# The first scan in two parts, the first rows from two queues, and POOL out of the heads and the last block

## The chip, the cores and the metric

The kernel runs on one core of one Trainium2 chip. The metric is the device time of one execution in microseconds; a comparison takes the median of several runs. Work is shared by five engines: PE (TensorE, matrix products, its weight loads shown as PEld), DVE (VectorE), ACT (ScalarE), POOL (GpSimd) and SP (SyncE, which in this kernel issues nearly all transfers). Each runs its own list of instructions in order and waits on semaphores for the others.

## The reference

Attention with a decay, and two feed-forward layers behind it:

```python
# q, k, v: (B 4, H 8, S 576, D 64); f: (B, H, S)
scores = scale * np.matmul(q, k.transpose(0, 1, 3, 2))
log_f = np.log(np.clip(f, 0.0001, 1.0))
cum = np.cumsum(log_f, axis=-1)
decay = cum[:, :, :, None] - cum[:, :, None, :]
scores = np.where(causal, -1000000000.0, scores + decay)
attn = np.exp(scores - np.max(scores, axis=-1, keepdims=True))
attn = attn / (np.sum(attn, axis=-1, keepdims=True) + 1e-09)
x = np.matmul(attn, v)                     # -> (2304 tokens, 512)
h = x @ moe_w_in                           # 512 x 2048
x = np.maximum(h, 0.0) ** 2 @ moe_w_out    # 2048 x 512
h = x @ moe2_w_in
g = np.where(h >= 1, h, np.where(h <= -1, 0.0, (h + 1) ** 2 / 4))
out = g @ moe2_w_out
```

The weights come as 64-bit floats; the kernel decodes them to 32-bit ones and splits each into a high and a low part, since its products are made of three matmuls (high by high, low by high, high by low).

## The kernel before

**Stages.** The tokens are cut into four blocks of columns. The first 256 rows of each sequence are "heads", computed in eight groups of four heads each by `attention32` (names with a q: s0q are the scores of group 0, E0q its exponentials, tr0q the transposed ones, av0q its second product). Groups 0 to 3 make the first block and run alone at the start, to about 48 us; groups 4 to 7 run between the feed-forward steps. The rest of each sequence is computed by `attention`, 32 tasks of one head each, between the feed-forward steps from 233 to 665 us. A feed-forward step is 24 matmuls of 128x512 of the first layer (L1129) or the second (L1180 to L1182). The last block of 768 tokens is computed by `last_block` with fewer products than the plain way: it makes sums of the weights and differences of the activations first. It does the first layer pair (mo=0) from 665 to 787 us and the second (mo=1) from 787 to the end. In each, eight pairs of activation chunks follow each other (names like G1_2: layer pair 1, chunk pair 2), 36 matmuls and more each.

**Start.** `setup` loads f (32 heads by 576), clips it (L535), takes the logarithm (L537) and sums it along the row with one scan (L538). The first 256 columns of all sums go to memory as `cumd` (L550). A group's tile QK holds queries and keys in 64 rows and the sums in two rows more, which the score matmul takes in with the rest. Those two rows of group 0 are copied straight from the scan's tile by `first_rows` (L554, two transfers); those of the other groups are read from `cumd` (L669). QK is cleared ahead of that (L606); K and Q of the later tasks are cleared at L564 and L565, by POOL or DVE. PE meanwhile runs 34 warm-up matmuls (L593). Behind the scores (L696) come, for each head, the row maximum and the shifted scores (L640, DVE), the exponential (L707, ACT), the sum and its reciprocal (L714, L715) and the normalising product (L730 on ACT, L731 on DVE, L732 on POOL).

**Second product of a task.** `attention` transposes its exponentials by transfers (PT), copies them to 32-bit tiles (pr) and multiplies them with V (L953): nine narrow matmuls of 320, 192 and 64 columns.

**Last block.** A pair's activations: h (L1335), ACT's two steps to r (L1354, L1356), DVE's step to G (L1359), then a split of G (gh and gl; ghl; L621, L624, L633) and subtractions of slots of G from each other (L1227, "G<-G"), and the products a, b, c (L1298 to L1300). Beside it `weight_sums` adds halves of the loaded second weights wo (wfs<-wo, twice 512 columns a pair) and makes four sums of 256 columns (sf), which are split into sum and stored. These adds go through `add`, which lets them run on DVE (L1227) or POOL (L1229):

```python
    def add(due, out, a, b, width, deps, bufs, sub=False, psum=False, slack=0.0, pool=True):
        op = ALU.subtract if sub else ALU.add
        alts = {"DVE": (dve_t(width), lambda: nc.vector.tensor_tensor(out(), a(), b(), op=op), *([] if psum else [True]))}
        if pool and not psum:
            alts["POOL"] = (pool2_t(width), lambda: nc.gpsimd.tensor_tensor(out(), a(), b(), op=op))
```

**What sets the order.** Every operation is entered with a due time, a price for each engine that may run it, what it depends on and its buffers. `Schedule.improve` simulates these lists with several weights, keeps the shortest result and fixes for every operation the engine and the place; `emit` writes the code in that order. It takes POOL's operations, and those of DVE that are marked with True, as exclusive of each other. Any changed price or due time may therefore reorder operations far away.

## Time and profile before

| | |
|---|---|
| time, three runs | 930.96, 932.15 (median), 935.03 us |
| profiled run | 933.11 us |
| its span | 931.3 us |
| mean granted clock of PE | 0.998 |
| busy in the span | PE 916.8, DVE 748.7, ACT 678.0, POOL 68.3 us |
| DMA | 247.38 MB, 266 GB/s on average |

The span reaches from the first to the last record of the profiled run; what is left to its time lies around it. A busy time is the sum of an engine's instructions. PE is the engine with next to no idle time, so a view of it is read for where it stands still; the other engines are read for what they do at those places.

### The profile page before, as it was taken

To read this page: it belongs to the slowest core of one execution; us is meant where nothing else is said; L and a number is where in the kernel's file an instruction comes from. 1 tells how busy PE (TensorE), PEld (TensorE's weight loads), DVE (VectorE), ACT (ScalarE), POOL (GpSimd) and SP (SyncE) were. 2 spreads that over 40 slices of the span, in tenths; PEclk is the share of its full clock that TensorE was granted. 3 is DMA by queue.
4 is the path that set the end of the run, shared out by engine and by line. 5 is a ranking of instruction groups with operands and counts; after the bars stand their busy time and mean duration, and the time that the engine had idled before them with its cause. 6 is when DMAs were issued, how large, how long until landed. Compare 5 with 4: busy or idle time off the path is not lost.

```text
span 931.3 us, 14313 instructions
## 1 busy us (share of the span) xinstructions
PE 916.8 (98%) x4674; PEld 799.3 (86%) x4674; DVE 748.7 (80%) x1711; ACT 678.0 (73%) x1354; POOL 68.3 (7%) x174
## 2 busy tenths in 40 slices
PE   7999999999999999999999999999999999989998
PEld 6788888877887888888888888888899999989998
DVE  8999999999858788888777778887676657788774
ACT  7998989897768777887777877886555555545553
POOL 4411001001000000000000000000000000322100
PEclk9999999999999999999999999999999999999999
DMA  7799999899898886998798888976697657756562
GB/s 216 257 356 397 347 399 332 324 359 332 295 300 249 257 273 219 320 262 236 242 295 261 279 247 236 262 218 179 205 307 266 218 219 255 253 196 225 214 226 89
DMA packets 132954, 247.38 MB, mean 266 GB/s; under 512 B 90512, under 2 KB 92720, under 8 KB 118096
## 3 DMA queue, kind: packets, MB, share of 16 engines
q1 hardware_dynamic: 132880, 246.47, 81.2%
q8 instruction: 37, 0.61, 0.3%
q14 instruction: 37, 0.30, 0.1%
HBM read 178.62 MB, written 46.84 MB: 242 GB/s over the span
## 4 chain that ended last, share of the span: by engine, by line
PE 89%; DVE 6%; ACT 2%; DMA 2%; issue 1%; SPq 0%; POOL 0%; DVEq 0%; ACTq 0%; POOLq 0%
PE h L1129 26%; PE h L1335 13%; PE acc L1180 9%; PE acc L1182 9%; PE acc L1181 9%; PE av L953 4%; PE s L847 2%; PE s L848 2%; PE b L1298 2%; PE b L1300 2%; PE b L1299 2%; PE c L1298 1%; PE c L1300 1%; PE c L1299 1%; PE a L1300 1%; PE a L1299 1%
## 5 line engine op out<-in xcount | busy, mean ns | idle before, releaser
L1129 PE MATMUL h<-x,whl 128*128 128x512 f32 x1128 | 286.1, 395 | 0.0
L1129 PEld LDWEIGHTS h<-x,whl 128*128 128x128 f32 x1128 | 208.9, 188 | 42.4 <-issue 0.5
L1180 PE MATMUL acc<-gh,whl 128*128 128x512 f32 x384 | 151.8, 395 | 0.0
L1182 PE MATMUL acc<-gl,whl 128*128 128x512 f32 x384 | 150.2, 391 | 0.0
L1181 PE MATMUL acc<-gh,whl 128*128 128x512 f32 x384 | 149.9, 390 | 0.0
L1182 PEld LDWEIGHTS acc<-gl,whl 128*128 128x128 f32 x384 | 72.1, 188 | 15.7
L1180 PEld LDWEIGHTS acc<-gh,whl 128*128 128x128 f32 x384 | 72.1, 188 | 14.6 <-issue 0.9
L881 ACT ACTIVATE E<-E,st 128x448 f32<-128x448 f32 (+2 forms) x96 | 63.5, 662 | 28.8 <-DVE st L640 22.7
L1181 PEld LDWEIGHTS acc<-gh,whl 128*128 128x128 f32 x384 | 72.2, 188 | 13.9
L633 DVE TENSOR_TENSOR gl<-g,gh 128x512 fp32r<-128x512 f32 x96 | 67.7, 706 | 15.8 <-PE acc L1182 9.9
L640 DVE CUSTOM_DVE_ANT_0 E<-s,mask 128x288 f32<-128x288 f32 (+2 forms) x128 | 59.8, 500 | 20.1 <-PE s L848 19.8
L1335 PE MATMUL h<-x_last,wi 128*128 128x384 f32 x384 | 72.7, 340 | 3.1 <-DVE G L1359 3.1
L923 DVE SCALAR_TENSOR_TENSOR PP<-E,st,PP 128x512 f16<-128x512 f32 (+2 forms) x128 | 70.0, 593 | 3.8 <-ACT PP L919 2.8
L1335 PE MATMUL h<-x,wi 128*128 128x384 f32 x384 | 72.0, 334 | 0.0
L919 ACT ACTIVATE PP<-E,st 128x512 f16<-128x512 f32 (+2 forms) x128 | 66.8, 590 | 6.9 <-DVE st L893 6.1
L1335 PEld LDWEIGHTS h<-x_last,wi 128*128 128x128 f32 x384 | 67.8, 190 | 4.3 <-DVE G L1359 4.1
L1335 PEld LDWEIGHTS h<-x,wi 128*128 128x128 f32 x384 | 67.1, 188 | 0.4
L624 DVE CAST pr<-PT 128x640 fp32r<-128x640 f16 (+2 forms) x93 | 32.0, 396 | 28.3 <-DMA PT<-PP 28.0
L1227 DVE TENSOR_TENSOR G<-G 128x384 f32<-128x384 f32 x64 | 37.7, 608 | 19.6 <-ACT G L1351 19.0
L953 PEld LDWEIGHTS av<-pr,vt 128*128 128x128 f32 x288 | 43.6, 188 | 4.1 <-ACT pr L621 1.0
L621 ACT ACTIVATE pr<-PT 128x640 fp32r<-128x640 f16 (+2 forms) x67 | 37.0, 602 | 13.4 <-DMA PT<-PP 12.3
L1156 ACT ACTIVATE r<-h,half 128x512 f32<-128x512 f32 x48 | 32.7, 681 | 18.9 <-PE h L1129 18.4
(352 smaller groups left out, 1796.7 us busy)
## 6 DMA issues: line engine op xcount, KB each, us to landing
whl<-scr SPq DMA_DIRECT2D x56, 1024.0 KB
raw<-in_w_dram SPq DMA_DIRECT2D x28, 1024.0 KB
scr<-whl SPq DMA_DIRECT2D x28, 1024.0 KB
wo<-scr SPq DMA_DIRECT2D x48, 512.0 KB
in<-in_qkv_dram SPq DMA_DIRECT2D x32, 608.0 KB
wi<-scr SPq DMA_DIRECT2D x32, 512.0 KB
whl<-scr SPq DMA_DIRECT2D x16, 512.0 KB
sum<-wfs SPq DMA_DIRECT2D x16, 512.0 KB
```

The lines of the kernel that those rows point to most:

```text
L633: alts["DVE"] = (dve_t(n), lambda: nc.vector.tensor_sub(out(), a(), b()), True)
L640: return nc.vector.tensor_tensor_reduce(out=out, in0=ps, in1=mask[:m, OFF - q0:OFF - q0 + n], scale=scale, scalar=3e38, op0=ALU.add, op1=A ...
L881: nc.scalar.activation(Ec.tile[:m, :e], Ec.tile[:m, :e], AF.Exp, scale=-1.0, bias=nmx(), accum_out=st.tile[:m, 1, ci:ci + 1])))}, [*tops, ...
L919: nc.scalar.activation(hi, x, AF.Copy, scale=r())
L923: nc.vector.scalar_tensor_tensor(lo, x, r(), hi, op0=ALU.mult, op1=ALU.subtract)
L953: nc.tensor.matmul(av.tile[:, c0:W], vt.tile[:, kc, :, :], dst()[:, i, :], start=(kc == 0 and i == 0), stop=(kc == NK - 1))
L1129: nc.tensor.matmul(ps.tile[:, :n], w.tile[:, 0, wi, kc * P:(kc + 1) * P], src.tile[:, kc, xi, :n], start=(kc == 0 and i == 0), stop=(kc == ...
L1180: nc.tensor.matmul(a.tile[:, :n], wh, gh.tile[:, :n], start=(fc == 0), stop=False)
L1181: nc.tensor.matmul(a.tile[:, :n], wl, gh.tile[:, :n], start=False, stop=False)
L1182: nc.tensor.matmul(a.tile[:, :n], wh, gl.tile[:, :n], start=False, stop=(fc == NFC - 1))
L1227: alts = {"DVE": (dve_t(width), lambda: nc.vector.tensor_tensor(out(), a(), b(), op=op), *([] if psum else [True]))}
L1335: nc.tensor.matmul(ps.tile[:, :n], W0.tile[:, j, wi, kc * P:(kc + 1) * P], src.tile[:, kc, xi, k * n:(k + 1) * n], start=(kc == 0 and i == ...
```

## The change

- Clip, logarithm and scan are each made in two parts, columns 0 to 256 and 256 to 576. The second scan starts from the last column of the first. What needs all columns (`cumhl`) hangs on the second.
- `first_rows` issues the first of group 0's two rows from SP and the second from ACT. The due time of the store to `cumd` goes from -98 to -80, behind that of the rows (-90).
- The memsets of Q and K are POOL's alone. The normalising product of the heads has no POOL any more (L732).
- `add` has no POOL any more, nor have the copies and subtractions that make x2, the input of the second layer pair in the last block (at L1405).
- The nine matmuls of a second product are sorted by width, narrow ones first but for the very first.
- The warm-up's price for the planner goes from 0.43 to 0.36 per matmul, and the planner knows a transfer by its price (a tuple), not by the engine, since ACT issues one now.

```diff
-            if e == "SP":
+            if type(cost) is tuple:
                 issue, size, hold, tail = cost
...
-            if o.eng == "SP":
+            if type(cost) is tuple:
                 end -= 0.65 + cost[0] + cost[1] + cost[3] - cost[2]
...
         sch.op(due + 90, {"POOL": (0.05, lambda: G.memset(half, 0.5))})
-        o3 = sch.op(due, {"DVE": (0.37, lambda: V_.tensor_scalar(
-            fr(), fr(), 1e-4, 1.0, op0=ALU.max, op1=ALU.min))}, [o1], [sb])
-        o4 = sch.op(due, {"ACT": (0.58, lambda: A.activation(lf(), fr(), AF.Ln))}, [o3, oh], [sb])
-        o5 = sch.op(-98.5, {"DVE": (0.67, lambda: V_.tensor_tensor_scan(
-            cum(), onesf(), lf(), 0.0, op0=ALU.mult, op1=ALU.add))}, [o4, o2], [sb])
-        sch.op(due, {"ACT": (1.4, lambda: A.activation(warm, warm, AF.Exp))}, [o4])
+        cut = [slice(0, HEAD), slice(HEAD, S)]
+        o3 = [sch.op(due, {"DVE": (0.15 + 0.1 * i, lambda c=c: V_.tensor_scalar(
+            fr()[:, c], fr()[:, c], 1e-4, 1.0, op0=ALU.max, op1=ALU.min))}, [o1], [sb]) for i, c in enumerate(cut)]
+        o4 = [sch.op(due, {"ACT": (0.32 + 0.05 * i, lambda c=c: A.activation(lf()[:, c], fr()[:, c], AF.Ln))}, [o3[i], oh], [sb])
+              for i, c in enumerate(cut)]
+        scan = lambda c, x: V_.tensor_tensor_scan(
+            cum()[:, c], onesf()[:, c], lf()[:, c], x(), op0=ALU.mult, op1=ALU.add)
+        o5 = sch.op(-98.5, {"DVE": (0.6, lambda: scan(cut[0], lambda: 0.0))}, [o4[0], o2], [sb])
+        o5b = sch.op(T_START + 14, {"DVE": (0.74, lambda: scan(cut[1], lambda: cum()[:, HEAD - 1:HEAD]))}, [o4[1], o5], [sb])
+        sch.op(due, {"ACT": (1.4, lambda: A.activation(warm, warm, AF.Exp))}, o4)
         hi = lambda: fr().bitcast(F32R)
         lo = lambda: lf().bitcast(F32R)
         o6 = sch.op(T_START + 16, {
             "ACT": (0.57, lambda: A.activation(hi(), cum(), AF.Copy)),
             "DVE": (0.37, lambda: V_.tensor_copy(hi(), cum())),
-        }, [o5], [sb], early=T_START + 12)
+        }, [o5b], [sb], early=T_START + 12)
         o7 = sch.op(T_START + 17, {"DVE": (0.67, lambda: V_.tensor_sub(lo(), cum(), fr()))}, [o6], [sb])
         o7 = [sch.op(due + 125, {"SP": (dma_t(73728), lambda i=i, b=b: nc.sync.dma_start(
             out=cumhl[:, i, :], in_=b()))}, [o], [sb], early=T_START + 12) for i, b, o in ((0, fr, o6), (1, lf, o7))]
-        o8 = sch.op(-98, {"SP": (dma_t(32768), lambda: nc.sync.dma_start(
+        o8 = sch.op(-80, {"SP": (dma_t(32768), lambda: nc.sync.dma_start(
             out=cumd, in_=cum()[:, :HEAD]))}, [o5], [sb])
 
-        def first_rows(row, out, due, deps):
-            return sch.op(due, {"SP": (dma_t(4096), lambda: nc.sync.dma_start(
+        def first_rows(row, out, due, deps, name):
+            eng = nc.sync if name == "SP" else nc.scalar
+            return sch.op(due, {name: (dma_t(4096, False), lambda: eng.dma_start(
                 out=out(), in_=cum()[row:row + QUAD, :HEAD]))}, [o5, *deps], [sb, QK[0]], early=0.0)
...
                 for r, x in ((64, 0.0), (4, -1.0 if n == "Q" else 1.0)):
-                    z = sch.op(due, {
-                        "POOL": (0.5, lambda t=t, r=r, x=x: G.memset(t[0:r, :].bitcast(F32), x)),
-                        "DVE": (0.5, lambda t=t, r=r, x=x: V_.memset(t[0:r, :].bitcast(F32), x)),
-                    }, [z])
+                    z = sch.op(due, {"POOL": (0.5, lambda t=t, r=r, x=x: G.memset(t[0:r, :].bitcast(F32), x))}, [z])
                 zs[n, i] = z
...
 
-        sch.op(-90, {"PE": (0.43 * WARM, lambda: mms(WARM))}, [id_op], [ps])
+        sch.op(-90, {"PE": (0.36 * WARM, lambda: mms(WARM))}, [id_op], [ps])
 
...
                 if i == 0:
-                    rows = [first_rows(row, lambda t=t: place(t, 0, QUAD), -90, [*cleared[0, 0], *cleared[0, 1]])
+                    rows = [first_rows(row, lambda t=t: place(t, 0, QUAD), -90, [*cleared[0, 0], *cleared[0, 1]], ("SP", "ACT")[t])
                             for t in range(2)]
...
                     "DVE": (dve2_t(e), lambda x=x, r=r: nc.vector.tensor_scalar(x(), x(), r(), None, op0=ALU.mult), True),
-                    "POOL": (pool_t(e), lambda x=x, r=r: nc.gpsimd.tensor_scalar(
-                        x(), x(), r(), 0.0, op0=ALU.mult, op1=ALU.add)),
                 }, [o_r], [Eb, st]))
...
         def mms():
-            for kc, c0, n, k, dst in moves:
-                for i in range(k):
-                    nc.tensor.matmul(
-                        av.tile[:, c0:W], vt.tile[:, kc, :, :], dst()[:, i, :],
-                        start=(kc == 0 and i == 0), stop=(kc == NK - 1))
+            parts = [(i, m) for m in moves for i in range(m[3])]
+            parts.sort(key=lambda p: (p[0] + p[1][0] > 0, p[1][2]))
+            for j, (i, (kc, c0, n, k, dst)) in enumerate(parts):
+                nc.tensor.matmul(av.tile[:, c0:W], vt.tile[:, kc, :, :], dst()[:, i, :],
+                                 start=(j == 0), stop=(j == len(parts) - 1))
 
...
 
-    def add(due, out, a, b, width, deps, bufs, sub=False, psum=False, slack=0.0, pool=True):
+    def add(due, out, a, b, width, deps, bufs, sub=False, psum=False, slack=0.0):
         op = ALU.subtract if sub else ALU.add
         alts = {"DVE": (dve_t(width), lambda: nc.vector.tensor_tensor(out(), a(), b(), op=op), *([] if psum else [True]))}
-        if pool and not psum:
-            alts["POOL"] = (pool2_t(width), lambda: nc.gpsimd.tensor_tensor(out(), a(), b(), op=op))
         return sch.op(due, alts, deps, bufs, slack)
...
                 sp1 = split(f"1_{nm}", tA + t_h + 1.5, gb, 0, [og[0, 0]], True)
-                o_t1 = add(tA + 3 * t_h + 1.5, slot(0), slot(1), slot(0), n, [og[0, 0], og[0, 1], sp1[3]], [gb], sub=True, pool=False)
-                o_t3 = add(te + 1.5, slot(1), slot(3), slot(1), n, [o_t1, og[1, 1], og[0, 1]], [gb], sub=True, pool=False)
+                o_t1 = add(tA + 3 * t_h + 1.5, slot(0), slot(1), slot(0), n, [og[0, 0], og[0, 1], sp1[3]], [gb], sub=True)
+                o_t3 = add(te + 1.5, slot(1), slot(3), slot(1), n, [o_t1, og[1, 1], og[0, 1]], [gb], sub=True)
                 sp5 = split(f"5_{nm}", te + 1.5, gb, 0, [o_t1])
-                o_t2 = add(te + 2, slot(0), slot(3), slot(0), n, [o_t1, sp5[3], og[1, 1]], [gb], sub=True, pool=False)
+                o_t2 = add(te + 2, slot(0), slot(3), slot(0), n, [o_t1, sp5[3], og[1, 1]], [gb], sub=True)
                 sp6 = split(f"6_{nm}", te + 2.5, gb, 0, [o_t2])
-                o_t4 = add(te + 3, slot(0), slot(2), slot(0), n, [o_t2, sp6[3], og[1, 0]], [gb], sub=True, pool=False)
+                o_t4 = add(te + 3, slot(0), slot(2), slot(0), n, [o_t2, sp6[3], og[1, 0]], [gb], sub=True)
                 g_op[c] = {"t4": o_t4, "t3": o_t3, "b21": og[1, 0], "b22": og[1, 1]}
...
                     o = o_r = add(due, t, ps, lambda: old.tile, n, dep, bufs, psum=True)
-                    o = sch.op(due + 0.5, copies(hi, t, n), [o], [buf, x2])
-                    x2_ops[d, k] = sch.op(due + 0.7, subs(lo, t, lambda: hi().bitcast(F32), n), [o], [buf, x2])
+                    o = sch.op(due + 0.5, copies(hi, t, n, "ACT DVE"), [o], [buf, x2])
+                    x2_ops[d, k] = sch.op(due + 0.7, subs(lo, t, lambda: hi().bitcast(F32), n, "DVE"), [o], [buf, x2])
                     return o_r
```

In the order of SP at the start (setup holds the scan's result, QK_199 is the tile of group 0, QK_237 that of group 1, raw are weights, vt values), before:

```order
L1022 DMA raw-2_228<-in_w_dram 128x512
L656 DMA QK_199<-in_qkv_dram 64x1024
L550 DMA cumd<-setup 32x256
L554 DMA QK_199<-setup 1x4x256 x2
L656 DMA QK_237<-in_qkv_dram 64x2048
L677 DMA vt0q<-in_qkv_dram 128x512
L1022 DMA raw-1_269<-in_w_dram 128x512
L669 DMA QK_237<-cumd 1x4x256 x2
L677 DMA vt1q<-in_qkv_dram 128x512
```

and after:

```order
L1022 DMA raw-2_228<-in_w_dram 128x512
L658 DMA QK_199<-in_qkv_dram 64x1024
L554 DMA cumd<-setup 32x256
L559 DMA QK_199<-setup 1x4x256
L658 DMA QK_237<-in_qkv_dram 64x2048
L679 DMA vt0q<-in_qkv_dram 128x512
L679 DMA vt1q<-in_qkv_dram 128x512
L671 DMA QK_237<-cumd 1x4x256 x2
L1022 DMA raw-1_284<-in_w_dram 128x512
```

The store to cumd stays ahead of the row; one row is left of two; raw-1 moves behind the rows of group 1.

The other row is in the order of ACT, after (before, none is there; low and wf are steps of decoding weights):

```order
L538 ACTIVATE setup<-setup 32x256
L538 ACTIVATE setup<-setup 32x320
L544 ACT_TABLE_LOAD
L544 ACTIVATE warm<-warm 128x1
L559 DMA QK_199<-setup 1x4x256
L1054 ACTIVATE low_260<-raw-2_228 128x512
```

It stands behind both logarithms, the load of the table for the exponential and its first use.

In the order of DVE at the start, from the clip to the first row maximum (L640 before, L642 after), before:

```order
L535 TENSOR_SCALAR setup<-setup 32x576
L606 MEMSET QK_199 64x2x256
L606 MEMSET QK_199 1x2x256
L538 SCALAR_TENSOR_TENSOR setup<-setup 32x576
L565 MEMSET K_0_144 64x576
L565 MEMSET K_1_145 64x576
L565 MEMSET K_0_144 4x576
L565 MEMSET K_1_145 4x576
L1065 TENSOR_SCALAR wf-2_257<-wf-2_257 128x512
L1067 TENSOR_SCALAR wf-2_257<-wf-2_257 128x512
L1070 ISA wf-2_257<-wf-2_257,low_262 128x1024
L640 ISA E0q_275,st0q_287<-s0q_274,mask 128x128
```

and after:

```order
L536 TENSOR_SCALAR setup<-setup 32x256
L536 TENSOR_SCALAR setup<-setup 32x320
L608 MEMSET QK_199 64x2x256
L540 SCALAR_TENSOR_TENSOR setup<-setup 32x256
L608 MEMSET QK_199 1x2x256
L540 SCALAR_TENSOR_TENSOR setup<-setup 32x320
L1061 TENSOR_SCALAR low_260<-raw-2_228 128x512
L642 ISA E0q_271,st0q_276<-s0q_270,mask 128x128
L642 ISA st0q_276 128x1
```

Two clips, two scans and one step of decoding stand ahead of the maximum now, where one clip, one scan, four memsets of K and three steps of decoding stood.

In the order of DVE in the last block, second layer pair, where the subtractions of chunk pairs 0 and 1 meet the activations of pair 2 (wfs and wo: weights of pair 4), before:

```order
L1227 TENSOR_TENSOR G_0_8904<-G_0_8904 128x384
L1359 SCALAR_TENSOR_TENSOR G_2_9170<-r_2_11_9197,h_2_11_9149 128x384
L1227 TENSOR_TENSOR G_1_9043<-G_1_9043 128x384
L1227 TENSOR_TENSOR G_0_8904<-G_0_8904 128x384
L1227 TENSOR_TENSOR G_1_9043<-G_1_9043 128x384
L1359 SCALAR_TENSOR_TENSOR G_2_9170<-r_2_00_9217,h_2_00_9193 128x384
L633 TENSOR_TENSOR gl_1_2_9248<-G_2_9170,gh_1_2_9235 128x384
L1227 TENSOR_TENSOR G_2_9170<-G_2_9170 128x384
L1359 SCALAR_TENSOR_TENSOR G_2_9170<-r_2_10_9243,h_2_10_9213 128x384
```

and after:

```order
L1227 TENSOR_TENSOR G_0_8907<-G_0_8907 128x384
L1357 SCALAR_TENSOR_TENSOR G_2_9175<-r_2_11_9200,h_2_11_9152 128x384
L1227 TENSOR_TENSOR G_1_9044<-G_1_9044 128x384
L1227 TENSOR_TENSOR G_0_8907<-G_0_8907 128x384
L1227 TENSOR_TENSOR wfs_4_9228<-wo_4_9149 128x512
L1357 SCALAR_TENSOR_TENSOR G_2_9175<-r_2_00_9220,h_2_00_9196 128x384
L1227 TENSOR_TENSOR sf_4_9237<-wfs_4_9228 128x256
L1227 TENSOR_TENSOR wfs_4_9228<-wo_4_9149 128x512
L635 TENSOR_TENSOR gl_1_2_9254<-G_2_9175,gh_1_2_9241 128x384
L1227 TENSOR_TENSOR G_2_9175<-G_2_9175 128x384
L1357 SCALAR_TENSOR_TENSOR G_2_9175<-r_2_10_9248,h_2_10_9216 128x384
L635 TENSOR_TENSOR ghl_1_2_9265<-G_2_9175,ghl_1_2_9265 128x384
```

The two adds wfs<-wo of pair 4, which were POOL's, now stand among them, one directly ahead of the step that makes G of pair 2, slot 00 (r_2_00).

## Rows read from the trace of the kernel before

**Rows 1.** The page, part 1: engine, busy us, share of the span, instructions.

```profile
PE 916.8 (98%) x4674; PEld 799.3 (86%) x4674; DVE 748.7 (80%) x1711; ACT 678.0 (73%) x1354; POOL 68.3 (7%) x174
```

**Rows 2.** Windows: from:to us, length, busy us per engine (instructions), clock, DMA.

```profile
9.20:22.00 12.80, 10.79 (x63) 7.45 (x65) 10.29 (x55) 10.02 (x39) 1.58 (x5) 1.00 1.02 278
22.00:48.50 26.50, 26.45 (x169) 19.39 (x166) 24.42 (x88) 24.92 (x73) 9.53 (x15) 1.00 0.82 262
48.50:233.00 184.50, 183.38 (x873) 148.74 (x872) 177.76 (x304) 163.15 (x267) 16.71 (x18) 1.00 0.95 356
```

**Rows 3.** The waits of PE: line, what it waited for, total, times, longest.

```profile
PE h L1335 <- DVE G L1359: 3.1, 2, 2.1
```

**Rows 4.** The timeline of the start: start, us, engine, line [idle before].

```profile
3.04 0.45 DVE L535 TENSOR_SCALAR setup<-setup 32x576 f32<-32x576 f32 x1
...
3.52 0.68 ACT L537 ACTIVATE setup<-setup 32x576 f32<-32x576 f32 x1 [1.29 <-DVE setup L535]
...
4.22 1.28 ACT L540 ACT_TABLE_LOAD   x1
...
4.82 1.35 DVE L538 TENSOR_TENSOR_SCAN setup<-setup 32x576 f32<-32x576 f32 x1
...
6.19 0.34 SPq L550 DMA_DIRECT2D cumd<-setup  x1
...
6.57 1.40 SPq L554 DMA_DIRECT2D QK<-setup  x2
...
9.20 2.86 PE L696 MATMUL s0q<-QK 128*128 128x128 f32 x16 [1.82 <-DMA QK<-setup]
...
9.66 0.69 DVE L1070 CUSTOM_DVE_ANT_0 wf-2_257<-wf-2_257,low 128x1024 uint16<-128x1024 uint16 x1
```

**Rows 5.** The chain that ended last: start, us, what.

```profile
10.46 5.39 DMA QK<-cumd
```

**Rows 6.** The timeline of the last block, second layer, at its two stalls.

```profile
814.33 1.29 POOL L1229 TENSOR_TENSOR wfs<-wo 128x512 f32<-128x512 f32 x1 [5.91 <-DMA wo<-scr]
814.45 1.45 DVE L624 CAST wfs<-sf 128x512 fp32r<-128x512 f32 x1
...
817.15 0.80 PE L1335 MATMUL h<-x_last,wi 128*128 128x384 f32 x3 [1.02 <-DVE G L1359]
...
826.47 2.83 POOL L1229 TENSOR_TENSOR wfs<-wo 128x512 f32<-128x512 f32 x2 [3.21 <-DMA wo<-scr]
...
826.66 4.06 DVE L1227 TENSOR_TENSOR G<-G 128x384 f32<-128x384 f32 x3
...
831.24 3.05 PE L1335 MATMUL h<-x_last,wi 128*128 128x384 f32 x9 [2.06 <-DVE G L1359]
```

**Rows 7.** Windows, as in rows 2, of two stretches of the last block.

```profile
831.50:834.80 3.30, 3.30 (x12) 3.30 (x12) 2.83 (x6) 1.76 (x4) 0.00 (x0) 0.50 0.62 225
851.90:863.40 11.50, 11.50 (x68) 11.45 (x68) 9.29 (x17) 6.55 (x13) 2.96 (x3) 1.00 0.67 242
```

**Rows 8.** Single lines: count, ns min/median/max, first and last start, forms.

```profile
L731 DVE TENSOR_SCALAR E3q<-E3q,st3q x4: 280/314/347, 34.9 to 35.5; 128x128 f32<-128x128 f32 x2, 128x256 f32<-128x256 f32 x2
...
L1229 POOL TENSOR_TENSOR wfs<-wo x8: 1279/1296/1610, 804.9 to 864.9; 128x512 f32<-128x512 f32 x8
...
L1227 DVE TENSOR_TENSOR G<-G x64: 549/557/1633, 675.5 to 901.8; 128x384 f32<-128x384 f32 x64
L1227 DVE TENSOR_TENSOR wfs<-wo x24: 683/685/917, 660.3 to 864.7; 128x512 f32<-128x512 f32 x24
L1227 DVE TENSOR_TENSOR sf<-wfs x24: 409/422/1403, 665.4 to 865.4; 128x256 f32<-128x256 f32 x24
```

**Rows 9.** The timeline of one second product.

```profile
256.28 1.30 PE L953 MATMUL av<-pr,vt 128*128 128x320 f32 x9
```

**Rows 10.** Waits of POOL and of DVE, as in rows 3.

```profile
POOL wfs L1229 <- DMA wo<-scr: 36.9, 5, 10.9
...
DVE wfs L1227 <- DMA wo<-scr: 1.2, 2, 0.8
```

## The prediction

> **What bounds the kernel now.** I read four views, from coarse to fine. The page gives each engine's share: PE is busy 98% of the span [rows 1], so the end moves only where PE idles, or where it runs slower than it could. The windows by stage say where that is. From 22 to 233 us PE has nothing left to give (26.45 of 26.50 us, then 183.38 of 184.50) [rows 2]; from 9.2 to 22 us it loses 2.0 us (10.79 of 12.80) [rows 2], and ahead of that it spins on warm-up matmuls until its first score. PE's list of waits names the largest stall of the rest: 3.1 us in two waits for G of line 1359 [rows 3], both in the last block. Then I read the timeline of those two places, line by line.
>
> *Start.* f passes clip (0.45 us), Ln (0.68), scan (1.35, from 4.82) [rows 4]. SP then issues the store of the first 256 columns (6.19), and behind it both row copies into QK, 1.40 us for the two, so done at 7.97. The first score matmul starts at 9.20, having waited 1.82 us for those rows [rows 4]: 1.23 us after the last issue. DVE's first row maximum cannot come before 10.35, since a decode op (L1070, 9.66 for 0.69 us) stands ahead of it [rows 4]. What comes next is the second group's rows, read back from the store: 5.39 us of the chain, until 15.85 [rows 5].
>
> *Last block.* At 826.47 POOL adds two pairs of weight halves, 2.83 us; beside it three DVE subtractions take 4.06 us, and the G that PE waits for stands behind them on DVE. PE resumes at 831.24 after 2.06 us idle [rows 6]. Behind that stall the granted clock is 0.50 of full speed (the lower level, 1.2 GHz) for 3.30 us [rows 7]. A smaller copy stands at 814: POOL's add of 1.29 us, DVE's cast of 1.45 beside it, PE idle for 1.02 us until 817.15 [rows 6].
>
> **The change, part by part.** The profiled run of before took 933.11 us (span 931.3 plus 1.8 around it), 0.96 above the median of 932.15. The terms are read in that run and taken off the median.
>
> *Scan in two parts, rows from two queues.* With 256 of 576 columns a DVE or ACT op keeps a fixed part, so I take half: clip 0.22, Ln 0.4, scan 0.65. The clip starts at 3.04 as before, both clips and one memset (two of them filled the 1.33 us between clip and scan, with Ln's end at 4.20 between them) then fill DVE until about 4.1, and the first scan ends near 4.75 instead of 6.17. SP's order still has the store ahead of row 0 (SP's rows in the order), so row 0 is issued after 0.34 for the store and 0.70 (half of 1.40): done at about 5.85. Row 1 is on ACT, behind the second Ln (to about 4.2) and the table load, 1.28 us [rows 4], with its warm-up: ready near 5.7, done near 6.4. The later of the two counts: 6.4 against 7.97. So the first score comes 1.6 us earlier, at about 7.6. Two issues on SP alone would end at 6.55; the second queue is worth 0.15. Cover lost: nothing, PE's warm-up matmuls end before that.
>
> The next stop also moves. In DVE's order the first maximum now stands behind one decode op (L1061) that needs only a load which has long landed, not behind the chain that ended in L1070 (its rows in the order). K's four memsets leave DVE for POOL. The load of raw-1 no longer stands between vt0q and the second group's rows (SP's rows in the order), so the transfer of 5.39 us [rows 5] shares the queues with less. I expect 0.6 us more from these, out of the 2.0 that PE idles in 9.2 to 22 us. Bounds: nothing, or all 2.0. Since PE is saturated from 22 us, what is gained reaches the end if DVE and ACT keep up. **Sum of the start: -2.2, between -1.0 and -3.6.**
>
> *No POOL in the heads.* Before, 16 of the 32 normalising steps of the first four groups are POOL's, 12 DVE's and 4 ACT's; now 20 and 12 (counted in the order of all three engines). A DVE one takes 0.31 us [rows 8]. Eight more on DVE are 2.5 us, against the K memsets gone and decode steps moved behind the first accumulating matmul; up to that place I count DVE's load changed by less than 0.3 us. So nothing in the sum; if the cover is gone, +2.5, as DVE is busy 24.42 of 26.50 us there [rows 2]. The trace says DVE at 92% has little room. The Trainium skill, "Perfetto Trace Analysis", section "Optimizing Scalar/DVE Operations", says that with a saturated DVE some work may go to ScalarE or GpSimd, which speaks against this part; it adds that DVE and GpSimd share a read port, so moving work between those two might not help. The case in which it does count is the second rival below.
>
> *No POOL in the last block.* Twenty-four POOL operations go: 8 adds of 512 columns, 1.30 us on POOL and 0.685 on DVE, 13 of 256 columns, 0.42 us on DVE [rows 8], and 3 on x_last (to ACT or DVE). That is 5.5 + 5.5 = 11.0 us more for DVE, less what its own operations no longer lose beside POOL. How this fits is read from one calm stretch: a pair takes 11.50 us there, DVE is busy 9.29, POOL 2.96 in three [rows 7]. One add of 0.685 and two of 0.42 make DVE 10.8 of 11.50. It fits with 0.7 us of room, so PE still sets the pace. What it gives back is the two stalls: 2.06 and half of the 3.30 us at the lower clock, 1.65, fall away if the subtractions take three times 0.56 again, their median [rows 8]; of the 1.02 I take 0.9, because the add that now precedes the G in question costs 0.7 where the cast lost 1.1. **Sum: -4.6, between 0 (the room is used up elsewhere) and -4.7.** The order shows the weak spot: an add of weights that waits for two loads now stands directly ahead of the G that the next product needs. Behind it on DVE queue that G, its split and the subtractions; ACT and then PE wait for these.
>
> What happened at 826 is a lock by all appearance: DVE's subtractions, both inputs in SBUF, last as long as POOL's add beside them. The Trainium skill, "SBUF — State Buffer", describes GpSimd and a two-port DVE operation as excluding each other outright instead of sharing. The rows agree (4.06 us where three take 1.7).
>
> *Second product by width.* Nine narrow matmuls go first to last in another order; in before nine take 1.30 us [rows 9], of which the narrow ones are limited by their weight loads, not by columns. Same set, same sum: 0, between -1 and +1 over 32 tasks. That copies are waited for earlier costs nothing while they end microseconds ahead.
>
> *Planner.* Warm-up cost and due times are only planner numbers, but every later instruction is placed anew. PE's small stalls in the saturated stretches come to about 1.2 us (0.05 and 1.12) [rows 2]; another order can have more. I put +0.5, between -1 and +2.5.
>
> Total: 932.15 - 2.2 - 4.6 + 0.5 = 925.9, so **926**.
>
> **Rivals.**
> 1. *The last block gives nothing* (930). DVE's room of 0.7 us a pair is used by waits for ACT between G and its split, so new short stalls take the place of the two long ones. For it: 10.8 of 11.50. Against: the old stalls came from inflated operations that the planner did not see. 932.15 - 2.2 + 0 = 930.
> 2. *The heads become DVE-bound* (928.5). Eight more steps cost 2.5: 926 + 2.5. For it: 92% DVE; against: equal total load.
> 3. *More from the start* (923.5). All 2.0 us of PE's idle time go and the clip and scan are cheaper: 926 - 2.5. For it: nothing else holds PE in 9.2 to 22; against: the transfer of 5.39 us is only started earlier.
> 4. *Slower* (940). In mo=1 DVE now waits in order for the late load of weights. POOL waited 36.9 us in 5 waits for wo [rows 10], one of 3.21 [rows 6], DVE only 1.2 in 2 [rows 10]. If DVE had to wait 1.6 to 3.2 us a pair, a pair would take 10.8 plus that, 0.9 to 2.5 over 11.50, seven times: +6 to +17, taken at +10: 932.15 - 2.2 + 10 = 940. It decides from 0.7 us of wait a pair. Against: DVE reaches its adds later than POOL did, when the load has landed.
> 5. *The change doesn't do what it says* (932). The store is still ahead of row 0, and the second queue saves 0.15. If the scan's halves too cost nearly their full price, the start gives nothing, and with rival 1 nothing is left.
>
> **How the numbers follow.** Forecast 0.55 (own range 923 to 929), rival 1 0.18, rival 2 0.06 (counted apart), rival 3 0.09, rival 4 0.07, rival 5 0.05. About 0.5% (4.66 us) is what a measurement of this kernel can tell from no change: faster is below 927.5, slower above 936.8. Below 927.5 lie most of the forecast (0.46) and rival 3 (0.09), together 0.55; between, the rest of the forecast, rivals 1, 2 and 5, 0.38; above, rival 4, 0.07. The range from 922 to 933 (both bounds of the start's sum and of the planner's, and the whole of rivals 1, 2 and 5) leaves out rival 4 and the far ends of rivals 3 and 5, some 0.15.
>
> **What would show it.** Right at the start: scan of 256 near 4.1 us, the last row issue at about 6.4, first score near 7.6, first accumulating matmul 2 us before 48.5. If the score comes early but the accumulating matmul does not, rival 2 holds. In the last block: no POOL in the timeline, subtractions G<-G at 0.56 each, no wait of PE for G above 0.5 us and no stretch at clock 0.50 behind it. If PE's waits for G are again 3 us in many short ones, rival 1; if DVE's list of waits shows wo by tens of microseconds, rival 4. The forecast is wrong first of all where the room of 0.7 us a pair is not enough.

## The result

The changed kernel takes 924.22 us (median; 923.52 to 926.06) against 932.28 in the same session: a ratio of 0.9915, interval 0.9898 to 0.9932. Beside the last experiments it was run again: 925.02, ratio 0.9925 (0.991 to 0.994). It is 7 to 8 us faster, inside the range, 1 to 2 us below the 926 of the forecast. The sum was right with two of its terms wrong: the start's was too large, and the planner's had the wrong sign.

The page of after, part 1 (engine, busy us, share of the span, instructions), and PE's waits:

```profile
PE 913.6 (99%) x4674; PEld 798.8 (87%) x4674; DVE 750.7 (81%) x1738; ACT 688.6 (75%) x1375; POOL 30.6 (3%) x129
```

```profile
PE tr0q L741 <- DVE E0q L733: 1.1, 1, 1.1
PE s1q L698 <- DMA QK<-cumd: 0.8, 1, 0.8
PE av7q L755 <- ACT pr7q L623: 0.7, 1, 0.7
PE av1q L755 <- ACT pr1q L623: 0.4, 1, 0.4
PE h L1333 <- DVE G L1357: 0.2, 1, 0.2
```

The 3.1 us for G of [rows 3] are 0.2, POOL's busy time is less than half, and PE runs through the last block. The timeline at the place of the long stall [rows 6] (start, us, engine, line):

```profile
820.79 0.55 DVE L1227 TENSOR_TENSOR G<-G 128x384 f32<-128x384 f32 x1
821.26 0.55 DVE L1357 SCALAR_TENSOR_TENSOR G<-r,h 128x384 f32<-128x384 f32 x1
821.73 1.02 DVE L1227 TENSOR_TENSOR G<-G 128x384 f32<-128x384 f32 x2
...
822.67 0.68 DVE L1227 TENSOR_TENSOR wfs<-wo 128x512 f32<-128x512 f32 x1
823.27 0.54 DVE L1357 SCALAR_TENSOR_TENSOR G<-r,h 128x384 f32<-128x384 f32 x1
```

One subtraction takes 0.55 and two together 1.02, so 1.57 for three, where three took 4.06; the added sum costs 0.68, and G follows in time. The start:

```profile
4.64 0.68 DVE L540 TENSOR_TENSOR_SCAN setup<-setup 32x256 f32<-32x256 f32 x1
5.35 0.34 SPq L554 DMA_DIRECT2D cumd<-setup  x1
5.35 1.18 ACTq L559 DMA_DIRECT2D QK<-setup  x1
...
5.72 0.75 SPq L559 DMA_DIRECT2D QK<-setup  x1
...
7.67 2.86 PE L698 MATMUL s0q<-QK 128*128 128x128 f32 x16
```

The first score is at 7.67 instead of 9.20 [rows 4]. Where the rest went is read from three marks on PE: the first accumulating matmul (48.53 before, 47.40 after), the first matmul of the last block (665.02, 661.36) and the span's end (931.3, 922.4). The three stretches changed by -1.1, -2.5 and -5.3 us.

### The profile page after: what moved, and what is told of

It reads as the page before. It is cut to its first block, busy times and chain, and to the rows that moved or that the text cites. A ratio compares the mean times of both kernels' runs of the same rounds, so it can differ in the third digit from the quotient of the medians.

```text
span 922.4 us, 14271 instructions
## 1 busy us (share of the span) xinstructions
PE 913.6 (99%) x4674; PEld 798.8 (87%) x4674; DVE 750.7 (81%) x1738; ACT 688.6 (75%) x1375; POOL 30.6 (3%) x129
## 4 chain that ended last, share of the span: by engine, by line
PE 90%; DVE 5%; ACT 2%; DMA 1%; POOL 1%; issue 1%; DVEq 0%; POOLq 0%; ACTq 0%
PE h L1129 27%; PE h L1333 13%; PE acc L1180 9%; PE acc L1182 9%; PE acc L1181 9%; PE av L954 4%; PE s L847 2%; PE s L848 2%; PE b L1296 2%; PE b L1298 2%; PE b L1297 2%; PE c L1296 1%; PE c L1298 1%; PE c L1297 1%; PE a L1297 1%; PE a L1298 1%
## 5 line engine op out<-in xcount | busy, mean ns | idle before, releaser
L1129 PE MATMUL h<-x,whl 128*128 128x512 f32 x1128 | 284.1, 393 | 0.0
L1129 PEld LDWEIGHTS h<-x,whl 128*128 128x128 f32 x1128 | 209.6, 188 | 42.5 <-issue 0.5
L881 ACT ACTIVATE E<-E,st 64x320 f32<-64x320 f32 (+2 forms) x96 | 63.4, 661 | 24.8 <-DVE st L642 19.5
L642 DVE CUSTOM_DVE_ANT_0 E<-s,mask 128x288 f32<-128x288 f32 (+2 forms) x128 | 59.8, 500 | 20.6 <-PE s L848 20.2
L1227 DVE TENSOR_TENSOR G<-G 128x384 f32<-128x384 f32 x64 | 34.4, 554 | 18.7 <-ACT G L1349 18.0
L1160 DVE SCALAR_TENSOR_TENSOR g<-r,h 128x512 f32<-128x512 f32 x48 | 32.8, 683 | 15.5 <-ACT r L1158 14.9
```

What stands on the lines that cost most here:

```text
L642: return nc.vector.tensor_tensor_reduce(out=out, in0=ps, in1=mask[:m, OFF - q0:OFF - q0 + n], scale=scale, scalar=3e38, op0=ALU.add, op1=A ...
L881: nc.scalar.activation(Ec.tile[:m, :e], Ec.tile[:m, :e], AF.Exp, scale=-1.0, bias=nmx(), accum_out=st.tile[:m, 1, ci:ci + 1])))}, [*tops, ...
L1129: nc.tensor.matmul(ps.tile[:, :n], w.tile[:, 0, wi, kc * P:(kc + 1) * P], src.tile[:, kc, xi, :n], start=(kc == 0 and i == 0), stop=(kc == ...
```

## Experiments

One profile is one execution, so the marks of all runs stand together; medians and ratios (with 95% intervals) are over several executions each, beside the kernel before on the same chip.

| kernel | first score | first acc | acc to last block | last block to end | median | ratio |
|---|---|---|---|---|---|---|
| before | 9.20 | 48.53 | 616.5 | 266.3 | 932.28 | 1 |
| e1_block_replan | 9.41 | 48.84 | 614.5 | 261.6 | 928.91 | 0.9965 (0.9946-0.9984) |
| e2_same_plan_dve | 9.20 | 48.45 | 616.3 | 261.3 | 927.48 | 0.9964 (0.9949-0.9980) |
| e4_start_replan | 8.85 | 48.81 | 616.1 | 264.4 | 933.86 | 1.0032 (1.0015-1.0050) |
| e11_heads_only | 9.21 | 51.15 | 615.8 | 264.7 | 933.75 | 1.0020 (1.0008-1.0033) |
| e12_four_rounds | 9.22 | 49.83 | 614.6 | 266.1 | 930.33 | 0.9984 (0.9972-0.9996) |
| e5_heads_pool_replan | 8.96 | 48.84 | 616.2 | 261.1 | 928.63 | 0.9971 (0.9957-0.9985) |
| after | 7.67 | 47.40 | 614.0 | 261.0 | 924.22 | 0.9915 (0.9898-0.9932) |
| e9_after_again | 7.97 | 47.61 | 614.1 | 261.8 | 925.02 | 0.9925 (0.9910-0.9940) |
| e3_same_plan_pool | 10.60 | 49.33 | 613.5 | 264.6 | 927.92 | 0.9964 (0.9951-0.9978) |
| e6_heads_pool_same_plan | 8.89 | 48.43 | 613.5 | 261.8 | 925.30 | 0.9925 (0.9896-0.9955) |
| e7_av_old_order | 9.16 | 47.88 | 614.3 | 261.7 | 925.63 | 0.9932 (0.9907-0.9957) |
| e8_store_behind | 9.01 | 47.90 | 614.5 | 261.4 | 925.37 | 0.9930 (0.9905-0.9956) |
| e10_raw_later | 7.67 | 50.36 | 613.7 | 261.1 | 928.46 | 0.9962 (0.9950-0.9975) |

**The last block.** Three kernels take the engine and the plan apart. e1 is the kernel before with only the last block's part of the diff, in `add` and in the copies and subtractions of x2:

```diff
-        if pool and not psum:
-            alts["POOL"] = (pool2_t(width), ...)
```

> The kernel before with one part of the change alone: no POOL in the last block, the planner free to place anew. Theory (POOL's adds hold DVE's operations with two SBUF inputs, and the two long stalls and the slow clock behind one of them are all that the last block loses): the second layer pair gives back 4.7 to 5.1 us, the rest of the kernel stays within 0.5 us of before, 927.4 us in all. Rival (the gain of the last block came with the new plan, of which the start and the body are a part): 930 to 932, PE still waits 2 us or more for G. Second rival (DVE is now the bound of the last block): PE's waits for G come back as many short ones, 930.

e2 keeps the plan of before and changes the engine behind the planner's back:

```diff
     sch.improve([p[0] for p in pools.values()], 6)
+    for o in sch.ops[n_before:]:          # operations of last_block
+        if o.eng == "POOL" and "DVE" in o.alts:
+            o.eng = "DVE"
```

> The kernel before with its plan kept to the letter, every operation at its old place in the order; only the last block's POOL operations run on DVE, at the places that their planned starts give them. Theory of the lock: the subtractions G<-G take 0.55 each again, PE's waits for G are under 1 us in sum, no stretch at clock 0.50, 927.5 us, as with a new plan. Rival (the plan matters, not the engine): DVE, for which these places were not planned, delays G itself, PE waits 2 to 4 us for G, 930 to 934.

e3 does the reverse to after's plan:

```diff
     sch.improve([p[0] for p in pools.values()], 6)
+    for o, fn in to_pool:                 # eight wfs<-wo of mo=1
+        o.alts["POOL"] = (0.0, fn)
+        o.eng = "POOL"
```

> The kernel after with its plan kept; only eight of the weight additions of 512 columns in the second layer pair (both of pairs 2 and 4, the first of pairs 3, 5, 6 and 7) run on POOL, at their places. Theory of the lock: whatever DVE operation with two SBUF inputs meets one of them lasts up to 1.3 us instead of 0.55, the maximum of G<-G is over 1 us, and PE waits 1 to 4 us for G again: 925.5 to 928.5. Rival (POOL and DVE do not hold each other; in before POOL was just a late supplier): G<-G stays at 0.56, DVE is relieved of 5.5 us, and the time stays at 924.2 or falls by up to 0.5.

With the old plan and DVE (e2) the last block takes 261.3 us as with a new plan (e1, 261.6), and e2's PE waits for G no more, as its theory said; e1 was expected 4.7 to 5.1 us better in the second layer pair, which holds against the profile of before, but its body is 2 us shorter too, and its median, 928.91, is above the 927.4 named. In e2 the subtractions of the second layer pair up to 890 us, by line (count, busy us, mean ns, idle before), are back at their length:

```profile
L1227 DVE TENSOR_TENSOR G<-G 128x384 f32<-128x384 f32 x30 | 16.0, 554 | 0.5
```

In e3 the stall is back. Its timeline at two of POOL's sums:

```profile
812.24 1.56 POOL L1242 TENSOR_TENSOR wfs<-wo 128x512 f32<-128x512 f32 x1 [6.95 <-DMA wo<-scr]
812.57 1.51 DVE L626 CAST wfs<-sf 128x512 fp32r<-128x512 f32 x1
...
815.33 1.86 PE L1338 MATMUL h<-x_last,wi 128*128 128x384 f32 x9 [1.30 <-DVE G L1362]
...
824.25 0.55 DVE L1362 SCALAR_TENSOR_TENSOR G<-r,h 128x384 f32<-128x384 f32 x1
824.31 2.85 POOL L1242 TENSOR_TENSOR wfs<-wo 128x512 f32<-128x512 f32 x2 [10.51 <-DMA wo<-scr]
824.71 2.87 DVE L1227 TENSOR_TENSOR G<-G 128x384 f32<-128x384 f32 x2
...
828.10 1.83 PE L1338 MATMUL h<-x_last,wi 128*128 128x384 f32 x9 [0.88 <-DVE G L1362]
```

Two subtractions that need 1.02 take 2.87 and end 0.42 us after POOL; the cast, 0.43 in after, takes 1.51. G of line 1362, with one input in PSUM, takes 0.55 beside POOL as always. The other traces with POOL in the last block (before, e4, e11, e12) agree: counted with e3, 22 subtractions G<-G start while a sum of POOL still has 0.3 us or more to run, and each ends 0.41 to 0.42 us behind that sum; 24 steps that make G start so, and none takes more than 0.56. So POOL's sums hold DVE's work between SBUF tiles, PE waits 2.8 us in three waits for it, and the kernel is 3 to 4 us slower than after. The rival (POOL merely late) falls. The Trainium skill, "SBUF — State Buffer", section "Who interferes with whom", says that a VectorE instruction with two SBUF inputs contends with a GpSimd one that reads SBUF, that a cast can do so in a two-port mode, and that one with at most one SBUF input outside these modes does not. The rows agree in all three: 2.87 for the subtractions, 1.51 for the cast, 0.55 for G.

The slow clock behind the stall was taken as part of it. It is there in some executions only. Windows behind the stall (from:to, length, busy of PE, PEld, DVE, ACT, POOL, then the granted clock), first e12 (PE idle for 1.77 us ahead of it), then e4 (1.96 us):

```profile
830.30:833.70 3.40, 3.40 (x12) 3.40 (x13) 2.68 (x6) 2.01 (x4) 0.00 (x0) 0.55 0.78 258
```

```profile
830.90:834.30 3.40, 3.40 (x20) 3.40 (x21) 2.70 (x6) 1.99 (x5) 0.00 (x0) 1.00 0.73 261
```

The kernels with POOL in the last block end 266.1 to 266.3 us behind its start where the clock fell (before, e12) and 264.4 to 264.7 where it did not (e4, e11, e3). Without POOL it is 261.0 to 261.8 in nine profiles. The term is 2.6 to 5.3 us; by the ratios of e1 and e2, 3.3. From the first matmul of the second layer pair to the end the groups part more clearly: 132.7 to 133.4 without POOL, 136.3 to 136.6 with it, 138.0 to 138.4 with it and the slow clock.

How often the clock falls is told by the mean granted clock of each execution, which stands on record, though not where it fell. Of the 71 executions of before beside the experiments, 39 have 0.998 or less, as the profiled one with its slow stretch has; they are 1.9 us slower on average than the others on the same chip. Of the 24 of after's plan (after, e6 to e9) it is one.

**The start.** e4 is the start's part of the diff alone, e5 after with L732 put back:

> The kernel before with the start's part alone: clip, logarithm and scan in two parts, rows from two queues, memsets of Q and K on POOL, the planner's price of the warm-up; POOL stays in the heads and the last block. Theory (the start's parts give 1.5 us to the first score by the smaller scan and the earlier issues): first score at 7.7, first accumulating matmul 1.1 to 2.2 us earlier than 48.5, and that much in the end, 930 to 931, if the body's plan loses nothing. Rival (the 1.4 us that the changed kernel lost again between 13 and 47 us come from taking POOL out of the heads): first accumulating matmul at 46.3 or earlier, PE does not wait 1.1 us for E0q. Rival of the scatter: the body from 48 to 665 us changes by 1 to 3 us either way, so the sum does not show the start's gain.

> The kernel after with one part undone: POOL may normalise in the heads again, as in before, and the planner places anew. Theory (the start alone was no gain because what POOL does there stands in DVE's way as in the last block): slower than after by 2 to 6 us, 926 to 930, PE loses more than in after between the first score and the first accumulating matmul, and DVE operations with two SBUF inputs are lengthened there. Rival (the heads' part is worth nothing, as the prediction had it): 924 to 925.5. Rival (it costs, since DVE is 92% busy there): under 923.5.

e4 is 0.3% slower than before, and none of its three expectations holds: its first score comes 0.35 us earlier, its first accumulating matmul is where it was, and a new plan has new stalls ("h <- ACT r", 1.3 us). e5 loses 3.6 to 4.4 us to after, in the span the first expectation named, but not where it said: from the first score to the first accumulating matmul it takes 39.9 us, e9 39.6. Of the loss 2.1 us are in the body (616.2 against 614.1), so again in the plan, and 1.2 ahead of it, of which 1.0 is the later first score.

e8 puts the store behind row 0, as the change's due times ask:

```diff
     sch.improve([p[0] for p in pools.values()], 6)
+    stores[0].start = firsts[0].start + 0.001
```

> The kernel after with its plan kept, but the store of the sums issued behind row 0 on SP, as the due times of the change ask for. Theory (the rows land when the loads issued ahead of them have drained, not by their own issue): the row is issued 0.35 us earlier, the first score stays where the loads let it, 7.6 to 10.6, time within 1 us of after. Rival (the issue is what holds the first score): first score at 7.3, 0.35 us less in all; the second group's rows, which wait for the store, come up to 0.7 us later.

Its rows are issued from SP and ACT at once, yet the score is at 9.01:

```profile
5.35 0.75 SPq L563 DMA_DIRECT2D QK<-setup  x1
5.35 1.18 ACTq L563 DMA_DIRECT2D QK<-setup  x1
...
9.01 1.33 PE L704 MATMUL s0q<-QK 128*128 128x128 f32 x7 [1.39 <-DMA QK<-setup]
```

Row 1's issue still ends at 6.53, as in after, and the score comes 1.3 us later. So the issue does not hold the score there. In the plans with two queues the first score follows the landing of raw-2, which its first decoding step on ACT shows (landing, score): after 6.75, 7.67; e9 7.10, 7.97; e5 7.63, 8.96; e6 7.67, 8.89; e8 7.78, 9.01; e7 7.80, 9.16; e4 7.92, 8.85; e3 8.51, 10.60. In before the landing can be 8.22 (e1) or 7.87 (e2) and the score is still 9.41 and 9.20, since there the rows are issued later. The times of single DMA packets, which the traces keep, agree: row 1, the only transfer in ACT's queue, is issued until 6.51 to 6.54 in every plan with two queues, but its last packet ends at 6.86 in after, 6.88 in e9, 7.59 to 7.97 in e4 to e8, and 8.84 in e3. The landing of raw-2 seems to go with the chip that ran the kernel: 7.10 to 7.43 in e9, e11 and e12, 7.63 to 7.80 in e5 to e8, 7.87 to 8.51 in e1 to e4, three chips. So does what the start gains at the first score: 1.2 us where e9 stands beside e11 and e12, but 0.35 to 0.56 where e4 stands beside e1 and e2, and e3 on that chip has it later than these. e10 takes raw-2 out of the way, behind row 0, with its first decoding steps behind the maxima:

```diff
     sch.improve([p[0] for p in pools.values()], 6)
+    stores[1].start = firsts[0].start + 0.01          # load of raw-2
+    for o, at in zip(dec, (11.505, 12.295, 12.465, 14.03)):
+        o.start = at
```

> The kernel after once more, beside the three others. Theory (its 7.67 for the first score was the early end of what the loads ahead of the rows allow): first score at 8.8 to 9.2 as in the variants that kept its plan, 925.3 us. Rival (7.67 is its rule): 7.6 to 7.8, 924.2 us.

> The kernel after with its plan kept, but for the first load of weights (raw-2, 512 KB), which SP issues behind row 0, and its first four decoding steps, which stand behind most of group 0's maxima and exponentials. Theory (the rows land when the loads issued ahead of them have drained, 1.2 us after raw-2): first score at 7.6 or earlier, 1.3 us and more ahead of after on the same chip; in the end 0.5 to 1.5 us less, as the decoding steps now cost DVE and ACT time in the busy stretch. Rival (the row's own issue and flight set the score): it stays where after has it, 8.8 to 9.2.

```profile
7.67 2.86 PE L704 MATMUL s0q<-QK 128*128 128x128 f32 x16 [0.49 <-DMA QK<-setup]
...
15.29 2.05 PE L704 MATMUL s1q<-QK 128*128 128x128 f32 x6 [2.04 <-DMA QK<-cumd]
```

The score is at 7.67, 1.14 us behind the last issue (6.53), as early as the best execution of after, and no earlier: that is what issue allows as far as one profile tells, and loads ahead add up to 2.9. But e9 had 7.97, between its two expectations, so the 1.3 us expected of e10 are 0.3, and the load now stands ahead of the second group's rows: PE waits 2.0 us for them, and behind that wait its clock is near half (0.54 in this window):

```profile
15.00:18.70 3.70, 3.41 (x14) 2.38 (x14) 1.71 (x11) 1.28 (x5) 0.00 (x0) 0.54 1.05 242
```

The first accumulating matmul is at 50.36, and the kernel is 3.4 us slower than after. All ten executions of e10 have a mean clock of 0.998 or 0.996 (927.1 and 929.1 us on average), all six of e9 have 1.0, so much of the loss goes with the clock. The load's place is a trade, and after has the better side.

**The heads.** e11 is the kernel before without L732:

> The kernel before with one part of the change alone: no POOL in the heads' normalising step, the planner free to place anew. Theory (POOL's steps themselves are worth nothing, the plan of the body is what differs): until 240 us as before, within 0.5 us; from 240 us to the start of the last block 421.8 to 424.8 us, as the new plan has it, 928.5 to 932. Rival (without POOL the heads are faster): first accumulating matmul 1 us or more ahead of 48.5.

Its first accumulating matmul is 2.6 us later, and the time 0.2% longer, above what either expectation named. The stretch of [rows 2] in e11, and ahead of it another, first in e11, then in before:

```profile
22.00:48.50 26.50, 25.35 (x164) 18.68 (x163) 25.61 (x108) 25.51 (x77) 4.40 (x2) 1.00 0.80 257
```

```profile
15.90:19.30 3.40, 3.37 (x13) 2.04 (x14) 1.75 (x8) 1.56 (x5) 0.00 (x0) 0.50 1.00 246
```

```profile
15.90:19.30 3.40, 3.21 (x21) 2.53 (x22) 1.93 (x11) 2.19 (x9) 0.00 (x0) 1.00 0.97 246
```

From 22 us DVE and ACT are full (25.61 and 25.51 of 26.50) and PE is not (25.35, so 1.15 us idle). But before that PE ran 3.4 us at half clock, 13 matmuls where before has 21, which costs up to 1.7 us. The plan, too, is another: 26 of the 32 steps are on DVE, where after has 20, and K's memsets still stand on DVE ahead of the score. So the 2.6 us have at least two causes, and e11 does not show that a missing cover is one. Ten of its 12 executions have a mean clock of 0.998 or less; the two others take 931.75 and 932.17, where before on the same chip takes 931.1 at such a clock. In after's plan the engine of these steps can be told apart from the rest: e6 (the 16 steps back on POOL) is the same as after in time:

> The kernel after with its plan kept; the 16 normalising steps of groups 0 to 3 that were POOL's in before run on POOL, each at its place. Theory (POOL is the slower engine there, and its steps and DVE's hold each other): first accumulating matmul 1 to 2 us later than with after, 925.5 to 926.5. Rival (DVE and ACT are the bound of the heads and are relieved of some 5 us): first accumulating matmul 0.5 to 1.5 us earlier, 923 to 923.8.

At 925.3 neither expectation shows in the time; the accumulating matmul is 0.8 us behind e9's, within what that mark varies.

**The order of the second product** (e7: the old loop over moves) is worth nothing that shows in the time:

> The kernel after with the nine matmuls of a second product in the old order, all else at its place. Theory (a narrow matmul costs its weight load in either order; one task takes 1.91 us in both traces): 924.2, within 0.5 of after. Rival (the order gives back 0.1 us a task): 926 to 928, or the same amount faster.

The 1.91 us of the expectation are in neither trace. The nine matmuls of a task take 1.37 to 1.39 us in after and 1.30 or 1.31 in e7, as in [rows 9], so a task is some 0.08 longer in the new order. The matmuls behind it are shorter: behind the task at 251 us, nine of the first layer take 2.22 us in after and 2.33 in e7. On the whole stretch that the next part measures (from 240 us to the last block), e7 takes 422.6 us and the other six executions of after's plan 421.8 to 422.2, so the new order may be worth 0.4 to 0.8 us there.

**The plan.** e12 is before with `improve(..., 4)` instead of 6, nothing else.

> The kernel before with nothing of the change, only four instead of six rounds of the planner, so another order of the same work. Theory (the body's 240 to 665 us depend on the plan by 2 to 3 us, whatever was changed): that stretch takes between 421.5 and 427 us and the whole differs from before by 1 us or more, either way. Rival (the plan matters by less than 0.5 us; the changed kernel's body is shorter for a reason in the change): 931 to 932, the stretch within 0.5 us of 424.7.

It is 0.16% faster, 1.5 us by the medians, so its theory holds: another order of the same work is enough to move the time. Counted from the 401st matmul of L1129 (240.19 in before) to the last block, e12 takes 423.98, e11 422.84, before 424.83, after 422.16, e9 422.09. But e1, whose order on every engine is before's until the last block, takes 422.90 and e2, likewise, 424.67. e2's list of PE's waits has what e1's lacks:

```profile
PE av L953 <- ACT pr L621: 0.6, 1, 0.6
PE s L847 <- DVE xs L972: 0.4, 1, 0.4
```

So the stretch varies by 2 us with one and the same order, and seven executions of after's plan all lie at the short end (421.8 to 422.6). That order does not run into these stalls; by how much this beats before's on average, some 1 to 2.5 us, these single profiles don't settle. The ratios, over many executions, bear it out: the last block alone has 0.9965 and 0.9964, after and the variants that keep its time 0.9915 to 0.9932, which leaves 3 to 5 us for start, heads and body together, and at the first accumulating matmul at most 1.1 of them are there.

## Why the prediction was right

**Last block, -4.6:** right in mechanism (e2, e3) and place, no new waits at the adds (DVE waits 1.3 us for wo in two waits, as in [rows 10]). The size is the upper end: the 3.0 us of stalls are given back in each comparison (3.0 to 3.3 in the second layer pair), the 1.65 of the slow clock only in executions that have it. DVE's room of 0.7 us a pair was enough, so rivals 1 and 4 fell. Rival 5 was half right: the store is still ahead of row 0, and that costs nothing (e8).

**Start, -2.2:** too large. The scan (0.68 against 0.65) and the last issue (6.53 against 6.4) come near; the scan's end is 5.32 against 4.75 forecast, as the two clips took 0.93 where 0.45 was counted and a memset follows them. Two steps failed. Row 1 did not wait for the table load: it is issued at 5.35, while the load runs (4.48 to 5.76), and takes 1.18 instead of 0.70. And 1.23 us from issue to score is a rule only while the loads ahead have drained, as in before; issued earlier, the rows meet them, and five of the eight profiles with two queues and raw-2 ahead have their score at 8.85 to 9.16. The 0.6 us more, too, failed as reasoned: the second group's matmuls do start 2 us earlier (at 13.5 to 14.0 in after, e9, e6, e7 and e8), but in the 13 us behind the score PE idles as much as before. In these windows of after (columns as above), which answer to the first two of [rows 2], PE idles for 2.09 us, where it idled for 2.01, and then for 0.54, where it idled for 0.05, with DVE busy 25.76 of 26.74:

```profile
7.67:20.66 12.99, 10.90 (x71) 8.24 (x71) 10.97 (x61) 10.70 (x43) 3.06 (x7) 1.00 0.99 281
20.66:47.40 26.74, 26.20 (x162) 18.88 (x160) 25.76 (x90) 24.71 (x73) 1.27 (x1) 1.00 0.81 247
```

Ahead of it, PE waits 1.1 us for E0q, as the normalising steps stand behind seven maxima in DVE's order. At the first accumulating matmul the gain is 0.6 to 1.1 us in after, e9, e7 and e8, 0.1 in e6, and none in e3.

**Heads, 0 with +2.5 if the cover is gone:** the 0 is right in after's plan (e6). The +2.6 of e11 at that mark looks like the other end, but the lower clock accounts for up to 1.7 of it, so what a missing cover costs was not shown. The sign named for rival 2, an early score without an early accumulating matmul, showed in part (1.5 us of gain at the score, 1.1 at the mark in after); that DVE's eight steps are the reason is open.

**Second product, 0:** right within its bounds, but not as reasoned: the order changes what a task and the matmuls behind it take (e7), 0.4 to 0.8 us in sum. **Planner, +0.5 between -1 and +2.5:** wrong side; -2.5 in the profile. That term had been read as PE's small stalls in a plan not yet seen; but the plan of before has stalls of its own there, which some executions meet and after's plan does not.

So the 6.3 us forecast and the 7 to 8 measured agree partly by chance: 1.1 to 2 us of the start did not come, and 2 to 3 us of the body came that had not been expected. Alone, the start's and the heads' parts made the kernel slower (e4, e11); together with the last block's they gain. That they need each other is not shown: each came with a plan of its own, with new stalls or more time at the lower clock. What in after's plan avoids the stalls stays open.

## What to carry to other kernels

Where a planner or scheduler counts GpSimd and VectorE as separate helpers, look for VectorE operations between SBUF tiles that end a fixed time (0.42 us here) behind a GpSimd one beside them: giving the work to the busy VectorE can be the faster choice if it has some room per step. A small transfer issued earlier gains only until it meets the bulk loads issued ahead of it. To judge one part of a change in a planned kernel, keep the plan and switch the engine or the place after planning; a part replanned alone measures the plan. Before a later mark is put down to an engine's load, read the granted clock of the stretch ahead of it.

## What was not expected of the hardware

ACT issues a transfer while its table load runs (5.35 us, the load from 4.48 to 5.76), but the issue takes 1.18 us beside one from SP of 0.75, against 1.40 for two in a row on SP. The clock fell to half behind PE idle times of 2.06 and 1.77 us, and stayed full behind one of 1.96. Near 15 us it fell in e11 and e12 behind waits of 0.8 to 0.9 us and some shorter ones, and stayed full in before, whose longest wait there was 0.9 us too. So in these traces the longest wait alone does not tell whether it falls.
